# Value product of a recurrent attention kernel: four 32-column tiles instead of two 64-column tiles

## The chip, the cores and the metric

The kernel runs on one core of one Trainium2 chip. The metric is the device time of one execution in microseconds (us); the time before is 1757.63 us, the median of 3 runs (1756.89 to 1763.15). The core's engines are TensorE (PE in the profile, its weight loads PEld), VectorE (DVE), ScalarE (ACT), GpSimd (POOL) and SyncE (SP), which issues nearly all DMAs.

## The reference, cut to what matters

A gated sum of two branches over 2048 tokens of width 640: branch A is attention with a recurrent memory, branch B a gated feed-forward layer.

```python
def _A_ref(x, mem0, Wq, Wk, Wv, Wo, seg_len):     # 32 heads of 192, 8 memory rows, segments of 32 tokens
    mem = mem0
    for s in range(n_seg):                         # 64 segments
        xs = x[:, s * seg_len:(s + 1) * seg_len, :].copy()
        h = jnp.concatenate([mem, xs], axis=1)     # 40 rows
        q = jnp.einsum('btd,dhe->bhte', h, Wq)
        k = jnp.einsum('btd,dhe->bhte', h, Wk)
        v = jnp.einsum('btd,dhe->bhte', h, Wv)
        scores = jnp.einsum('bhqe,bhke->bhqk', q, k) * scale
        scores = jnp.where(mask[None, None], scores, -1000000000.0)
        p = _softmax(scores, axis=-1)
        o = jnp.einsum('bhqk,bhke->bhqe', p, v)    # the value product
        o = jnp.einsum('bhte,hed->btd', o, Wo)
        mem = o[:, :M, :].copy()
        outs.append(o[:, M:, :])
...
return g * a + (1 - g) * b
```

The memory rows of one segment come out of the segment before, so the 64 segments run one after another. All tensors are bf16.

## The kernel before

The kernel first computes the feed-forward branch in four blocks of 512 tokens and parks it in device memory, together with the columns of q and k that the last 8 tokens of each segment need. That ends at about 189 us of the profile. Then come the 64 segments of about 24.5 us each.

The weights of the attention do not all fit in the on-chip memory: in each segment a part of them is exchanged by loads on SP's queue (`load_piece`, L599), each of which waits until TensorE has done with what lies in the place.

The heads are worked in four groups of eight, called octets. `PROG` (L506) is an order written out by hand in which a segment's pieces follow one another on TensorE: projection steps `("g", n, k)`, transpositions of rows `("tq", o)` and `("tk", o)`, scores `("sc", o)`, softmax `("ex", o)`, transposition of the probabilities `("pt", o)`, value product `("pv", o)`, output projection `("wo", o, half)`, and pieces `("lf", ...)`, `("le", ...)`, `("vb", ...)` for the rows of later segments. Each engine runs its own list in that order; `_Sched.finalize` sets semaphore waits where a piece reads or writes what another engine wrote or read. If a TensorE piece has several waits, some are put ahead of the last matmuls of the piece before it.

Most matmuls of a segment use 32 of the 128 columns of the array: four stand side by side at column positions 0, 32, 64 and 96, each with its own moving data (projections L1046 and, with kept weights, L226; L884 and L1019 for the later segments' rows; the output projections L1206 and L1229; the transposition of the probabilities L1144 and L1149). The scores (L1087, L1095, L1100) have 40 columns and stand in two halves of 64.

The value product of an octet is `pv_oct` (L1165). Four pairs of heads lie in the partitions, and three parts `c` of 128 value columns each are multiplied with the transposed probabilities of two halves `i`: a wide matmul over all 160 columns (4 pairs x 40 rows, L1177) with the segment's own values `v`, and a narrow one of 64 columns (4 x 16, L1179) that adds the values `vl` of the last 8 tokens. Each takes 64 value columns as its weights, so two of them, `i` = 0 and 1, stand side by side in the array. That makes 12 matmuls and 12 weight loads per octet, 256 octets in all. Ahead of it stands ScalarE's evacuation of the transposed probabilities (L1162; for the last octet L1156 and L1158) and of the values (L1069). Behind it ScalarE evacuates the result (L1188; a third of the last octet goes to VectorE, L1193) for the output projection.

In the hand-written order the product of octet 0 lies between the scores of octet 1 and the transposition of octet 1; that of octet 1 directly behind the scores of octet 2 and ahead of the transposition of octet 2; that of octet 2 ahead of the scores of octet 3; that of octet 3 ahead of the last output projection, from whose result VectorE makes the memory rows of the next segment (L1371, L1375).

Of the kernel before, what the change touches and what calls it, by code (L numbers as in the profile page):

```python
# [231 lines left out]
def _build(nc, A_x, A_mem0, A_Wq, A_Wk, A_Wv, A_Wo, seg_len, w_gate, w_up, w_down,  # L232
# [18 lines left out]
    R = L + M  # L251
    XA = L - M
# [14 lines left out]
    S_ = _Sched(nc)  # L267
# [27 lines left out]
    NVB, NUB = 2, 2  # L295
# [33 lines left out]
    ps = nc.alloc_psum_tensor("ps", [128, 8, 512], F32)  # L329
# [3 lines left out]
    o = wsA_base - wsB_total  # L333
# [6 lines left out]
    o = wsA_base  # L340
# [4 lines left out]
    o = ffn_base  # L345
# [10 lines left out]
    def sreg(o, nbytes, plo=0, phi=128):  # L356
        return Rg("sb", o, o + nbytes, plo, phi)
# [39 lines left out]
    r_v = [sreg(wsB_off["v"] + b * 768, 768) for b in range(NVB)]  # L397
# [8 lines left out]
    PTm = PT[:, 0:PTW].rearrange("p (i t r) -> p i t r", t=4, r=R)  # L406
    PTl = PT[:, PTW:PTW + 128].rearrange("p (i t r) -> p i t r", t=4, r=16)
    r_PT = sreg(wsB_off["PT"], 2 * (PTW + 128))
# [23 lines left out]
    o = ffn_base - sum(fp_sz.values())  # L432
# [48 lines left out]
    r_ps = [Rg("ps", b, b + 1) for b in range(8)]  # L481
# [45 lines left out]
    def octet(s, i):  # L527
        return i if s % 2 == 0 else NOCT - 1 - i
# [35 lines left out]
    o = 0  # L564
# [71 lines left out]
    def load_residents(cls, pick=lambda key: True):  # L636
        for key in first:
# [7 lines left out]
           reads=[r_ident], writes=[r_ident])  # L645
    def asel(ap, reg, pattern, base, cm, fill):
# [12 lines left out]
           reads=[r_elw], writes=[r_elw])  # L659
# [19 lines left out]
    for h in range(NH):  # L679
        for w_, sb_, rw_, nm in ((w_gate, wg_sb, r_wg, "wg"), (w_up, wu_sb, r_wu, "wu")):  # L680
            S_.add("sp", lambda e, h=h, w_=w_, sb_=sb_: e.dma_start(
                sb_[h], w_.rearrange("(p k) f -> p k f", p=128)[:, :, FH * h:FH * (h + 1)]),
                writes=[rw_[h]], dma_sem="%s%d" % (nm, h))
# [228 lines left out]
    for n, (g, o) in enumerate(units):  # L912
# [7 lines left out]
        if g == 0:  # L920
            S_.add("pool", lambda e, o=o, b=b: e.tensor_copy(out=stg[o // 2][:, o % 2], in_=lst[b][:, 0]), reads=[r_lst[b]], writes=[r_stgh[o // 2][o % 2]],
                   name="stg s0 o%d" % o)
# [74 lines left out]
    def misc_bank(s, group=9):  # L997
        tick[0] += 1
        ok = [b for b in (0, 1, 2, 3) + ((LB,) if s % 4 in (1, 2) or s % 4 == 3 and group < 3 else ()) + ((OB,) if group < 2 else ()) if b not in bk_of.values() and b not in lb.values()]
        b = min(ok, key=lambda b: misc[b])  # L1000
        misc[b] = tick[0]
        return b

    def apx(ap, dims):
        return bass.AP(ap.tensor, ap.offset, [list(ap.ap[0])] + [list(d) for d in dims])
# [159 lines left out]
    def pv_oct(s, o):  # L1165
        A = misc_bank(s)
        B = misc_bank(s) if o in USPLIT else A
        oc = octet(s, o)
        v, vl, u = v_sb[o % NVB], vl_sb[oc], uT[o % NUB]
        ru = r_uTp[o % NUB]  # L1170
        W = 4 * R

        def half(c, i):
            full = ps[64 * i:64 * i + 64, B if c == 2 else A, W * c:W * c + W]
            part = full.rearrange("p (t r) -> p t r", r=R)[:, :, XA:R]
            e0 = 128 * c + 64 * i
            return [lambda e: e.matmul(full, v[:, e0:e0 + 64], PTm[:, i], start=True, stop=False,  # L1177
                                       tile_position=(0, 64 * i), skip_group_check=True),
                    lambda e: e.matmul(part, vl[:, e0:e0 + 64], PTl[:, i], start=False, stop=True,  # L1179
                                       tile_position=(0, 64 * i), skip_group_check=True)]  # L1180

        fns = [x for c in range(3) for y in zip(half(c, 0), half(c, 1)) for x in y]
        if s % 4 == 0:
            S_.add("pe", fns[:2], reads=[r_v[o % NVB], r_PT], writes=[r_ps[A]], name="PV s%d o%d" % (s, o))
            del fns[:2]
        S_.add("pe", fns, reads=[r_v[o % NVB], r_vl[oc], r_PT], writes=[r_ps[A]] + ([r_ps[B]] if B != A else []), name="PVa s%d o%d" % (s, o))
        na = 2 if o in USPLIT else 3
        S_.add("act", lambda e: e.activation(  # L1188
            out=apx(u[:, 0, 0, :], [[R, na], [3 * R, 4], [1, R]]),
            in_=ps[:, A, 0:na * W].rearrange("p (c t r) -> p c t r", t=4, r=R), func=ACTF.Copy),  # L1190
            reads=[r_ps[A]], writes=[ru[0]] if na == 2 else ru, name="uT evac s%d o%d" % (s, o))
        if na == 2:
            S_.add("dve", lambda e: e.tensor_copy(out=u[:, :, 2, :], in_=ps[:, B, 2 * W:3 * W].rearrange("p (t r) -> p t r", r=R)),  # L1193
                   reads=[r_ps[B]], writes=[ru[1]], name="uT mid s%d o%d" % (s, o))
        q = s % 4
        S_.add("pool", lambda e: e.tensor_copy(  # L1196
            out=uTl[:, 12 * oc:12 * oc + 12, M * q:M * q + M].rearrange("p (t c) i -> p t c i", c=3), in_=u[:, :, :, L:R]),
            reads=[r_uT[o % NUB]], writes=[r_uTl[oc]], name="uTl s%d o%d" % (s, o))
# [91 lines left out]
    def segment(s):  # L1290
# [3 lines left out]
        for n, item in enumerate(PROG):  # L1294
# [29 lines left out]
            elif kind == "pv":  # L1324
                pv_oct(s, i)
            elif kind == "lf":
                if i == q and unit(s, item[2]):
                    if item[3] == 0:
                        for m in range(2):
                            lb[item[2], m] = misc_bank(s)  # L1330
                    for m in range(2):
                        LBK[m] = lb[item[2], m]
                    left_mm(*unit(s, item[2]), item[3], unit_piece)
            elif kind == "vb":
                if q == 3 and g + 1 < NG:
                    if i == 0:
                        lb["v"] = misc_bank(s)
                    vl_mm(s + 1, i)
            elif kind == "le":
                if i == q and unit(s, item[2]):  # L1340
                    if n > n_wo:
                        post.append(item[2:])
                    else:
                        left_evac(s, *item[2:])
            else:
                held = wo_part(s, item)
                if i == 2 and item[2] == 0 and q == 0 and g > 0:
                    outl_store(g - 1)
                if item == items[-1] and s + 1 < NSEG:
                    stg_load(s + 1, 1)  # L1350
                if q == 3 and item != items[-1]:
                    wo_left(s, held)
# [118 lines left out]
```

## Time and profile before

| what | before |
|---|---|
| device time, median of 3 | 1757.63 us (1756.89 to 1763.15) |
| the profiled execution, span from first to last instruction | 1765.1 us (no other time of it is given) |
| mean granted TensorE clock | 0.994 |
| TensorE busy, matmuls | 1623.9 us, 92% |
| weight loads busy | 809.5 us, 46% |
| VectorE, ScalarE, GpSimd busy | 54%, 45%, 18% |
| value product, wide (L1177) | 1536 matmuls and weight loads, matmul mean 243 ns |
| value product, narrow (L1179) | 1536 matmuls and weight loads, matmul mean 193 ns |
| moved by DMA | 499.57 MB, mean 283 GB/s |

A matmul's own duration covers its way through the array, so successive matmuls overlap: four 384-wide matmuls side by side last 0.34 us each, and the next four start 0.16 us after them. For what a piece costs in TensorE's stream, the distance from start to start is to be read. A line of the timeline gives the start in us from the span's beginning, the time to the end of its group, engine, line, operation, the used rows and columns of the array, the moving operand, and how many; a bracket gives idle time of the engine before it and what ended it. "issue" in such a bracket means that the engine waited for nothing that the profile shows. In the page, the row "DMA" gives the busy share of the 16 DMA engines in tenths for 40 slices of the span, and the row that begins with "PE 71%" is the chain of work that ended last, by engine.

### The profile page before, as it was taken

To read this page: it belongs to the slowest core of one execution; us is meant where nothing else is said; L and a number is where in the kernel's file an instruction comes from. 1 tells how busy PE (TensorE), PEld (TensorE's weight loads), DVE (VectorE), ACT (ScalarE), POOL (GpSimd) and SP (SyncE) were. 2 spreads that over 40 slices of the span, in tenths; PEclk is the share of its full clock that TensorE was granted. 3 is DMA by queue.
4 is the path that set the end of the run, shared out by engine and by line. 5 is a ranking of instruction groups with operands and counts; after the bars stand their busy time and mean duration, and the time that the engine had idled before them with its cause. 6 is when DMAs were issued, how large, how long until landed. Compare 5 with 4: busy or idle time off the path is not lost.

```text
span 1765.1 us, 80301 instructions
## 1 busy us (share of the span) xinstructions
PE 1623.9 (92%) x39162; PEld 809.5 (46%) x31501; DVE 960.0 (54%) x2932; ACT 802.8 (45%) x1835; POOL 320.0 (18%) x1099
## 2 busy tenths in 40 slices
PE   9999999999999999999999989999999998999887
PEld 4554444444444444454444444454444444454444
DVE  2222655556555655555555655555555655655554
ACT  3222544545444544444444544444444544445443
POOL 1100111111112112111212111111211121121211
PEclk9999999999999999999999999999999999999999
DMA  9814987888778887888788887879787886879776
GB/s 335 295 48 157 329 313 250 320 313 288 280 269 311 299 308 253 315 290 319 281 280 293 296 293 250 314 285 323 279 280 275 311 310 241 312 282 327 283 275 238
DMA packets 271311, 499.57 MB, mean 283 GB/s; under 512 B 105304, under 2 KB 132208, under 8 KB 270960
## 3 DMA queue, kind: packets, MB, share of 16 engines
q1 hardware_dynamic: 267832, 491.34, 78.3%
q8 instruction: 276, 4.52, 1.0%
q10 hardware_dynamic: 3128, 3.09, 0.6%
q14 instruction: 75, 0.61, 0.1%
HBM read 473.22 MB, written 21.11 MB: 280 GB/s over the span
## 4 chain that ended last, share of the span: by engine, by line
PE 71%; DVE 15%; DMA 6%; issue 4%; ACT 4%; DVEq 0%; SPq 0%; ACTq 0%
PE ps L1046 20%; PE ps L226 15%; PE ps L1206 8%; DMA arena<-in_A_Wo_dram 5%; PE ps L1177 3%; PE ps L804 3%; PE ps L801 3%; PE ps L884 3%; PE ps L1100 3%; PE ps L819 2%; PE ps L1087 2%; DVE ps L1114 2%; DVE arena L1112 2%; PE ps L1095 2%; PE ps L1229 2%
## 5 line engine op out<-in xcount | busy, mean ns | idle before, releaser
L1046 PE MATMUL ps<-arena 128*32 128x384 bf16 x9940 | 723.0, 329 | 42.4 <-DVE arena L1375 34.4
L226 PE MATMUL ps<-arena 128*32 128x384 bf16 x7680 | 595.4, 328 | 7.9 <-DVE arena L1215 3.5
L1046 PEld LDWEIGHTS ps<-arena 128*32 128x32 bf16 x9940 | 257.5, 97 | 365.3 <-issue 226.0
L1080 DVE STREAM_TRANSPOSE arena<-arena 128x384 bf16<-128x384 bf16 x512 | 270.8, 557 | 150.8 <-ACT arena L1066 149.2
L1066 ACT ACTIVATE arena<-ps 128x384 bf16<-128x384 f32 x512 | 236.2, 489 | 211.6 <-PE ps L1046 196.3
L1206 PE MATMUL ps<-arena 128*32 128x320 bf16 x6144 | 293.6, 301 | 13.9 <-issue 13.4
L1124 ACT ACTIVATE ps<-ps 104x160 f32<-104x160 f32 x256 | 71.9, 281 | 293.4 <-DVE ps L1114 293.4
L1206 PEld LDWEIGHTS ps<-arena 128*32 128x32 bf16 x6144 | 163.5, 97 | 74.0 <-issue 19.4
L1112 DVE TENSOR_REDUCE arena<-ps 104x4 f32<-104x160 f32 x256 | 83.0, 324 | 165.8 <-PE ps L1100 164.6
L941 POOL COPY arena<-arena 128x96 bf16<-128x96 bf16 x256 | 70.3, 275 | 513.4 <-PE ps L1100 444.2
L1188 ACT ACTIVATE arena<-ps 128x480 bf16<-128x480 f32 (+1 forms) x256 | 137.0, 535 | 43.8 <-PE ps L1179 39.6
L1196 POOL COPY arena<-arena 128x96 bf16<-128x96 bf16 x256 | 68.3, 267 | 441.1 <-ACT arena L1188 357.3
L1162 ACT ACTIVATE arena<-ps 128x448 bf16<-128x448 f32 x192 | 104.2, 543 | 96.7 <-PE ps L1149 96.4
L1069 ACT ACTIVATE arena<-ps 128x384 bf16<-128x384 f32 x256 | 125.1, 489 | 20.9 <-PE ps L1046 16.3
L1177 PE MATMUL ps<-arena 128*64 128x160 bf16 x1536 | 123.1, 243 | 12.5 <-ACT arena L1162 6.9
L1126 DVE TENSOR_REDUCE arena<-ps 104x4 f32<-104x160 f32 x256 | 83.0, 324 | 92.5 <-ACT ps L1124 92.5
L1177 PEld LDWEIGHTS ps<-arena 128*64 128x64 bf16 x1536 | 80.8, 109 | 91.6 <-issue 31.7
L884 PE MATMUL ps<-arena 128*32 128x384 bf16 x1280 | 111.4, 330 | 2.2 <-issue 2.0
L1179 PE MATMUL ps<-arena 128*64 128x64 bf16 x1536 | 104.8, 193 | 4.1 <-issue 4.1
L891 DVE STREAM_TRANSPOSE arena<-arena 128x384 bf16<-128x384 bf16 x128 | 73.7, 576 | 31.6 <-ACT arena L889 27.8
L1215 DVE TENSOR_TENSOR arena<-ps,arena 64x160 f32<-64x160 f32 x160 | 50.8, 317 | 72.3 <-ACT arena L1212 61.6
L1114 DVE TENSOR_TENSOR ps<-ps,arena 104x160 f32<-104x160 f32 x256 | 85.0, 332 | 8.8
(84 smaller groups left out, 1819.2 us busy)
## 6 DMA issues: line engine op xcount, KB each, us to landing
arena<-in_A_Wk_dram SPq DMA_DIRECT2D x335, 384.0 KB, 7.1
arena<-in_A_Wv_dram SPq DMA_DIRECT2D x335, 384.0 KB, 9.1
arena<-in_A_Wo_dram SPq DMA_DIRECT2D x205, 480.0 KB, 6.4
arena<-in_A_Wq_dram SPq DMA_DIRECT2D x209, 384.0 KB, 5.4
arena<-left_qk_scratch SPq DMA_DIRECT2D x126, 96.0 KB, 2.8
left_qk_scratch<-arena SPq DMA_DIRECT2D x49, 192.0 KB, 2.3
left_qk_scratch<-arena SPq DMA_DIRECT2D x30, 96.0 KB, 5.7
ffn_b_scratch<-arena ACTq DMA_DIRECT2D x16, 160.0 KB, 4.4
```

Source lines behind the costliest of these rows:

```text
L226: return e.add_instruction(mybir.InstMatmult(name=nm, start_tensor_calc=like["start"], stop_tensor_calc=stop, tile_size=(128, 32), tile_po ...
L884: fns.append(lambda e, outp=outp, rhs=rhs, j=j: e.matmul(outp, lhs, rhs, start=(k == 0), stop=(k == KT - 1), tile_position=(0, 32 * j)))
L1046: fns.append(lambda e, outp=outp, rhs=rhs, j=j: e.matmul(outp, lhs, rhs, start=(k == 0), stop=(k == KT - 1), tile_position=(0, 32 * j)))
L1066: S_.add("act", lambda e, m=m, bk=bk: e.activation(out=rows_sb[m], in_=ps[:, bk, 0:384], func=ACTF.Copy), reads=[r_ps[bk]], writes=[r_rows ...
L1069: S_.add("act", lambda e, i=i, bk=bk: e.activation(out=v_sb[i % NVB].rearrange("p (c n) -> p c n", c=3), in_=ps[:, bk, 0:384].rearrange("p ...
L1080: S_.add("dve", lambda e: e.transpose(out=dst[:, :, 0:L], in_=rows_sb[m].rearrange("p (c r) -> p c r", r=L)), reads=[r_rows[m]], writes=[r ...
L1112: S_.add("dve", lambda e: e.tensor_reduce(out=mxs, in_=S3, axis=AX.X, op=ALU.max), reads=[rb], writes=[rst], name="smax max")
L1114: S_.add("dve", lambda e: e.tensor_tensor(out=S3, in0=S3, in1=mxb, op=ALU.subtract), reads=[rb, rst], writes=[rb], name="smax sub")
L1177: return [lambda e: e.matmul(full, v[:, e0:e0 + 64], PTm[:, i], start=True, stop=False, tile_position=(0, 64 * i), skip_group_check=True), ...
L1179: lambda e: e.matmul(part, vl[:, e0:e0 + 64], PTl[:, i], start=False, stop=True, tile_position=(0, 64 * i), skip_group_check=True)]
L1188: S_.add("act", lambda e: e.activation(out=apx(u[:, 0, 0, :], [[R, na], [3 * R, 4], [1, R]]), in_=ps[:, A, 0:na * W].rearrange("p (c t r) ...
L1206: fns.append(lambda e, i=i, t=t, j=j, gv=gv: e.matmul(ps[32 * j:32 * j + 32, bank, 0:2 * DJ].rearrange("p (h n) -> p h n", h=2), lhs2[i], ...
```

## The change

In `pv_oct` the two 64-column tiles of each matmul become four 32-column tiles. Each part `c` now issues four wide matmuls, at column positions 0, 32, 64 and 96, and then four narrow ones; the moving operand and the place in the result are unchanged, the weights are 32 value columns each. An octet has 24 matmuls and 24 weight loads. In segments whose number is a multiple of four the first piece, which doesn't wait for `vl`, holds four matmuls instead of two. No other function is touched, and the other engines' instructions keep their order.

```diff
-        def half(c, i):
-            full = ps[64 * i:64 * i + 64, B if c == 2 else A, W * c:W * c + W]
-            part = full.rearrange("p (t r) -> p t r", r=R)[:, :, XA:R]
-            e0 = 128 * c + 64 * i
-            return [lambda e: e.matmul(full, v[:, e0:e0 + 64], PTm[:, i], start=True, stop=False,
-                                       tile_position=(0, 64 * i), skip_group_check=True),
-                    lambda e: e.matmul(part, vl[:, e0:e0 + 64], PTl[:, i], start=False, stop=True,
-                                       tile_position=(0, 64 * i), skip_group_check=True)]
-
-        fns = [x for c in range(3) for y in zip(half(c, 0), half(c, 1)) for x in y]
+        def strips(c):
+            full, part = [], []
+            for i in range(2):
+                for h in range(2):
+                    lo = 64 * i + 32 * h
+                    acc = ps[lo:lo + 32, B if c == 2 else A, W * c:W * c + W]
+                    e0 = 128 * c + lo
+                    full.append(lambda e, acc=acc, e0=e0, i=i, lo=lo: e.matmul(
+                        acc, v[:, e0:e0 + 32], PTm[:, i], start=True, stop=False, tile_position=(0, lo), skip_group_check=True))
+                    part.append(lambda e, acc=acc, e0=e0, i=i, lo=lo: e.matmul(
+                        acc.rearrange("p (t r) -> p t r", r=R)[:, :, XA:R], vl[:, e0:e0 + 32], PTl[:, i], start=False, stop=True,
+                        tile_position=(0, lo), skip_group_check=True))
+            return full + part
+
+        fns = [x for c in range(3) for x in strips(c)]
         if s % 4 == 0:
-            S_.add("pe", fns[:2], reads=[r_v[o % NVB], r_PT], writes=[r_ps[A]], name="PV s%d o%d" % (s, o))
-            del fns[:2]
+            S_.add("pe", fns[:4], reads=[r_v[o % NVB], r_PT], writes=[r_ps[A]], name="PV s%d o%d" % (s, o))
+            del fns[:4]
```

## The prediction

> **What bounds the kernel now.** I read the page first: the busy shares, the DMA and queue rows, the chain.
>
> ```profile
> span 1765.1 us, 80301 instructions
> PE 1623.9 (92%) x39162; PEld 809.5 (46%) x31501; DVE 960.0 (54%) x2932; ACT 802.8 (45%) x1835; POOL 320.0 (18%) x1099
> ...
> DMA  9814987888778887888788887879787886879776
> ...
> q8 instruction: 276, 4.52, 1.0%
> ...
> PE 71%; DVE 15%; DMA 6%; issue 4%; ACT 4%; DVEq 0%; SPq 0%; ACTq 0%
> ```
>
> TensorE is busy in 92% of the span and holds 71% of the chain: what shortens its stream counts unless something else ends the wait. The q8 row matters as much. In it 276 packets carry 4.52 MB. 39162 matmuls and 31501 weight loads are 70663 instructions, 256.0 to each of the 276 packets: the stream comes in 16 KB blocks of 256, so more instructions mean more blocks.
>
> Then the timeline of PE, around one value product and around one transposition of the probabilities.
>
> ```profile
> 926.58 0.34 PE L226 MATMUL ps<-arena 128*32 128x384 bf16 x4
> 926.85 0.26 PE L1177 MATMUL ps<-arena 128*64 128x160 bf16 x2
> 926.94 0.20 PE L1179 MATMUL ps<-arena 128*64 128x64 bf16 x2
> 926.97 0.24 PE L1177 MATMUL ps<-arena 128*64 128x160 bf16 x2
> 927.04 0.20 PE L1179 MATMUL ps<-arena 128*64 128x64 bf16 x2
> 927.07 0.24 PE L1177 MATMUL ps<-arena 128*64 128x160 bf16 x2
> 927.14 0.20 PE L1179 MATMUL ps<-arena 128*64 128x64 bf16 x2
> 927.27 0.35 PE L1046 MATMUL ps<-arena 128*32 128x384 bf16 x4
> 927.44 0.34 PE L226 MATMUL ps<-arena 128*32 128x384 bf16 x4
> ```
>
> ```profile
> 903.54 0.34 PE L226 MATMUL ps<-arena 128*32 128x384 bf16 x4
> 903.70 0.21 PE L1144 MATMUL ps<-arena 104*32 104x80 bf16 x4
> 903.74 0.23 PE L1149 MATMUL ps<-arena 104*32 104x128 bf16 x4
> 903.80 0.34 PE L1046 MATMUL ps<-arena 128*32 128x384 bf16 x4
> ...
> 907.26 0.22 PE L1144 MATMUL ps<-arena 104*32 104x80 bf16 x4 [0.30 <-DVE arena L1131]
> ```
>
> Four 32-column matmuls of 384 take 0.16 us from group to group, and a 32-column group of another kind (L1144) starts at that distance too. The 64-column L1177 starts 0.27 us after L226, and L1046 0.13 us after the last L1179, though 64 columns cost only 0.03 us between the pairs. So changing the tile's width costs about 0.1 us each way. L1144 at 907.26 waits for VectorE's softmax: an earlier TensorE gains nothing there.
>
> Last, a gap named "issue".
>
> ```profile
> 470.53 0.24 PE L1177 MATMUL ps<-arena 128*64 128x160 bf16 x1
> 472.21 0.26 PE L1177 MATMUL ps<-arena 128*64 128x160 bf16 x1 [1.44 <-issue]
> ```
>
> TensorE stops 1.44 us inside the value product, waiting for no semaphore. From 189 us on there are 55 such gaps over 30 ns, 34.7 us together. Counted along matmuls and weight loads they lie multiples of 256 apart: those at 466.0, 472.2, 523.6 and 547.7 us stand before instructions 14746, 15002, 17306 and 18330, in four different lines. TensorE waits there for the next block. All other idle time of TensorE there is 94 us.
>
> **The change part by part.** I work in distances between starts, medians over the trace, in ns; 256 value products (64 segments, four octets).
>
> *Removed: the width changes.* Last matmul before to first L1177: 256 after a 384-wide group, against 153 between two such groups: 103 lost. The product of octet 1 follows the scores (L1100) at 106, and from L1100 to the 32-column L1046 it is 106 too, so nothing is won there. Last L1179 to the next group 122, against 25 from L1179 to L1177: 97 lost.
>
> *The block.* First to last start is now 298. The new block is three 160-wide and three 64-wide groups of four. A four-group of 160 exists (L1229: 3+3+3+59, so 68); the 64-wide one lies between 27 (64/384 of the 160 that a 384-wide group takes) and 35 (25 plus three starts). So the block to the next start costs 3 x 68 + 3 x 27..35 = 285 to 309; I take 300. Now that part is 298 + 122 = 420: 120 saved (111 to 135), plus 103 on entry for three of four octets. A segment saves 3 x 223 + 120 = 789, and 64 of them 50 us (48 to 54).
>
> *What does not reach the end.* The third octet's transposition waits for VectorE in 58 of 64 segments (23.8 us): octet 1's product lies between that octet's scores and this wait, so 58 x 0.12 = 7 us vanish. 15 products of octet 2 wait for ScalarE (L1162) and drain meanwhile: 1.5. The later transpositions wait 48 times, and take perhaps half of octet 2's saving: 5. Left 36, I take 35; bounds 25 and 50. Octet 3's product feeds a serial chain (evacuation, Wo), so its saving passes on. The wait that each product has on ScalarE or VectorE stands before the same first matmul; with four in that first piece instead of two nothing new queues behind it. No transfer and no instruction of the other engines moves.
>
> *Added: instructions.* 12 matmuls and 12 weight loads per product are 24 x 256 = 6144 instructions, 24 blocks: 276 to 300. A segment goes from 1060 instructions (4.14 blocks) to 1156 (4.52). Lower bound: each block stalls as now, 34.7 us / 253 = 0.14 us, 24 x 0.14 = 3 us. But stalls depend on how long a block lasts. The packet records of q8 in the trace put the start of the fetch of the next block 2.9 us (median) after the running block's first instruction when the 16 DMA engines are full, 1.1 us when they are nearly idle; the next block's first instruction runs at least 2.36 us after that start. A block that lasts under some 5.3 us with DMA full is thus in danger. The 149 blocks that begin with DMA full, sorted by duration without the stall:
>
> - under 4.8 us: 7 blocks, all stalled, mean 1.35 us
> - 4.8 to 5.2: 31, mean 0.33
> - 5.2 to 5.6: 35, mean 0.14
> - 5.6 to 6.0: 60, mean 0.05
> - longer: 16, mean 0.05
>
> The sum is 28.5 us. With 1060/1156 of the old work and 35 of 1570 us saved, a block lasts 0.90 of what it did, and there are 1.09 times as many. The rows move down a class: 8 x 1.8 + 34 x 1.35 + 38 x 0.6 + 65 x 0.2 + 17 x 0.1 = 98 us (the values between classes read off the list, 1.8 extrapolated). That is +69; a tenth falls where TensorE would have waited anyway: +62. Upper bound 100 (all 162 blocks at 0.8 us, less the 28.5). I take 62, not 3: the list is this kernel's own behaviour at the durations that the blocks will have.
>
> On this the Trainium skill says otherwise: Runtime: NRT & Kernel Launch, Instruction fetch mechanics, has the next 16 KiB block fetched while the present one runs and the crossing "mostly hidden". By it the sum would end at the 35 us saved; the 55 gaps speak against it.
>
> *Sum.* -35 + 62 = +27 us. On the profiled execution's span, 1765.1 (the page gives no other time of it, and it is 0.4% above the median of the runs), that is 1792; on the median 1757.63 it is 1785.
>
> **The rivals.**
>
> *The fetch stays hidden (faster).* Place: the block boundaries; price: -35 + 3 = -32 us, so 1726. For it: the fetch starts at 1.1 us when DMA is idle, and a stall of TensorE lets DMA run dry, so stalls may limit themselves; boundaries also fall elsewhere in the program. Against it: DMA is nine tenths busy in most slices and the short blocks all stall. It decides when the stalls grow by less than 35 us, under about 0.25 us for each block.
>
> *They cancel.* Stalls grow by 27 to 43 us: 1749 to 1766.
>
> *A floor for each matmul (slower still).* If every matmul took 25 ns, the product would last 600 instead of 300: 153 + 600 against 256 + 298 + 122, +77 ns, 20 us on 256, and with less dense blocks perhaps 20 us of new stalls: 1798. For it: L1095's two-tile pairs of 40 columns take 28 ns, not 17. Against it: L1144's four start 3 ns apart and the next group 0.04 us after the first.
> TensorE: Matmul & The Clock Gate (the Trainium skill), Wait — 56ns, not 53.3ns?, states that floor of about 25 ns between starts; the L1144 rows, four tiles side by side, do not show it.
>
> *The drain does not belong to the width* and stays: then only the block changes, nothing is saved, and +55 us of stalls gives 1813. Against it: L1144's undelayed start.
>
> **How the numbers follow.** Stalls outgrow the saving: 0.54, likeliest 1785, own range 1767 to 1812. Fetch hidden: 0.23, 1726, 1710 to 1749. Cancel: 0.13. Floor 0.05, drain stays 0.05. A measurement of this kernel can tell about 0.5% (8.8 us) from no change: slower 0.54 + 0.05 + 0.05 = 0.64, same 0.13, faster 0.23. The range leaves a tenth out at either end: half of the faster case, below 1729, and the top of the slower ones, above 1815.
>
> **What would show it.** In the profile after: 42234 matmuls, 34573 weight loads, q8 with 300 packets and 4.92 MB. The product from the group before to the group after: about 0.45 us where it was 0.68. Gaps named issue: near 97 us where they were 34.7, again 256 instructions apart, most in the stretches where DMA is full. The third transposition's wait longer by about 0.1 us. It is wrong if those gaps stay under 70 us, or if L1144 and Wo wait so little that stalls of TensorE pass on in full.

## The result

The changed kernel takes 1834.8 us (median of 4 runs, 1828.99 to 1835.47) against 1760.39 us for the kernel before beside it: a ratio of 1.0398, 95% interval 1.0354 to 1.0443. It is 74 us slower. The forecast was slower, 1785 us, with a range from 1729 to 1815: the direction and the mechanism came out, the size did not.

The rows of the page that answer to those shown of the kernel before:

```profile
span 1833.7 us, 86445 instructions
PE 1606.6 (88%) x42234; PEld 830.1 (45%) x34573; DVE 959.2 (52%) x2932; ACT 804.8 (44%) x1835; POOL 321.6 (18%) x1099
...
DMA  9816887878777877878777887878777887778786
...
q8 instruction: 300, 4.92, 1.1%
...
PE 69%; DVE 16%; issue 9%; ACT 4%; DMA 1%; DVEq 0%; SPq 0%; ACTq 0%
```

TensorE is busy 17 us less than before, in a span that is 69 us longer. The instruction queue q8 has its 24 blocks more, and "issue" went from 4% of the chain to 9%.

The timeline of PE around one value product of the changed kernel (L1180 is the wide matmul, L1182 the narrow one):

```profile
913.35 0.34 PE L226 MATMUL ps<-arena 128*32 128x384 bf16 x4
913.52 0.34 PE L1046 MATMUL ps<-arena 128*32 128x384 bf16 x4
913.68 0.24 PE L1180 MATMUL ps<-arena 128*32 128x160 bf16 x4
913.75 0.20 PE L1182 MATMUL ps<-arena 128*32 128x64 bf16 x4
913.78 0.24 PE L1180 MATMUL ps<-arena 128*32 128x160 bf16 x4
913.85 0.20 PE L1182 MATMUL ps<-arena 128*32 128x64 bf16 x4
913.88 0.24 PE L1180 MATMUL ps<-arena 128*32 128x160 bf16 x4
913.95 0.20 PE L1182 MATMUL ps<-arena 128*32 128x64 bf16 x4
913.97 0.34 PE L1046 MATMUL ps<-arena 128*32 128x384 bf16 x4
```

The product now starts 0.16 us after the group before it, as any group does, lasts 0.29 us to the next group, and the next group follows at once. From the start of the group before to the start of the group after it takes 0.45 us, as forecast, where it was 0.69 in the kernel before. On the array the change does just what the start distances promised.

The waits of TensorE's matmuls, longest first (us in total, times, longest):

```profile
PE ps L1046 <- DVE arena L1380: 34.0, 48, 1.4
PE ps L1211 <- issue: 23.1, 25, 1.7
PE ps L1144 <- DVE arena L1131: 22.8, 48, 0.8
PE ps L1182 <- issue: 20.6, 15, 2.4
PE ps L1046 <- issue: 19.9, 19, 1.8
PE ps L1180 <- issue: 11.1, 13, 1.5
PE ps L884 <- issue: 10.3, 11, 1.6
```

The same view of the kernel before had, for comparison:

```profile
PE ps L1046 <- DVE arena L1375: 34.4, 48, 1.2
PE ps L1144 <- DVE arena L1131: 25.0, 65, 0.7
PE ps L1206 <- issue: 13.4, 14, 2.0
...
PE ps L1229 <- DMA arena<-in_A_Wo_dram: 6.1, 10, 2.3
PE ps L1046 <- issue: 5.4, 8, 1.3
PE ps L1177 <- issue: 4.8, 6, 1.5
PE ps L1179 <- issue: 4.1, 6, 1.3
```

The waits for VectorE (L1380, in the old numbering L1375, and L1131) are about what they were; the wait for the weights Wo (L1229) is gone. What grew is "issue": in the product (old L1177 and L1179, new L1180 and L1182), but also in the projections (L1046, L884) and the output projection (old L1206, new L1211), which the change did not touch. From 189 us on these gaps are 116.7 us in 130 places, where they were 34.7 us in 55; again they stand multiples of 256 instructions apart.

A gap shows less than what a late block costs. In the changed kernel:

```profile
918.87 0.34 PE L1046 MATMUL ps<-arena 128*32 128x384 bf16 x3
920.01 0.34 PE L1046 MATMUL ps<-arena 128*32 128x384 bf16 x1 [0.81 <-issue]
```

The fourth matmul of a group starts 1.13 us after the third, where it normally starts 0.003 us after it; the gap is 0.81 us, because the third's own 0.34 us are still counted as work. So I count a stall at each block boundary as the start distance there, less the median distance of the same pair of lines elsewhere. Added up over the segments by the place in the segment (us from VectorE's L975, or the same line in the other kernels, which ends a segment's output; all stalls over 0.06 us):

```
                0-10   10-14  14-18  18-22  22-     sum
before           4.9     4.4   23.3   24.7    1.6    59
after            9.1    45.8   53.7   35.1   15.5   159
```

The 16 DMA engines are full (a mean share of 0.9 to 1.0 over the segments) from about 2.5 to 18 us of a segment in both kernels, then fall to 0.8 at 19 us, 0.5 at 21 us and 0.2 from 22 us on. The stalls have grown by 100 us, 72 of them at 10 to 18 us. Those that stand later mostly follow blocks that were entered earlier: 93% of the stall time in the changed kernel, and 91% in the kernel before, lies behind blocks in whose first 3 us the DMA engines are over 0.9 busy. (Such blocks are called blocks that begin with DMA full in what follows.) The span has grown by 68.6 us, so everything else together has become 32 us shorter.

The packets of q8 tie these stalls to the fetch. In the changed kernel the next block's packet starts 3.1 us (median) after a block that begins with DMA full is entered, and 1.1 us after it where DMA is under 0.2 busy; the packet itself takes 1.0 us in both. It is the start that is late. At the 118 boundaries with a stall of more than 0.5 us the first matmul runs 2.4 us (median, nine tenths between 2.3 and 2.6) after the start of the last packet: the end of the stall follows the packet at an almost fixed distance.

### The profile page after: what moved, and what is told of

It reads as the page before. It is cut to its first block, busy times and chain, and to the rows that moved or that the text cites. A ratio compares the mean times of both kernels' runs of the same rounds, so it can differ in the third digit from the quotient of the medians.

```text
span 1833.7 us, 86445 instructions
## 1 busy us (share of the span) xinstructions
PE 1606.6 (88%) x42234; PEld 830.1 (45%) x34573; DVE 959.2 (52%) x2932; ACT 804.8 (44%) x1835; POOL 321.6 (18%) x1099
## 4 chain that ended last, share of the span: by engine, by line
PE 69%; DVE 16%; issue 9%; ACT 4%; DMA 1%; DVEq 0%; SPq 0%; ACTq 0%
PE ps L1046 18%; PE ps L226 14%; PE ps L1211 9%; PE ps L884 3%; PE ps L804 3%; PE ps L1100 3%; PE ps L801 3%; PE ps L1180 3%; DVE ps L1114 2%; PE ps L1087 2%; DVE arena L1112 2%; PE ps L1095 2%; PE ps L819 2%; DVE arena L1126 2%; DVE arena L891 2%
## 5 line engine op out<-in xcount | busy, mean ns | idle before, releaser
L1046 PE MATMUL ps<-arena 128*32 128x384 bf16 x9940 | 733.1, 328 | 55.7 <-DVE arena L1380 34.0
L226 PE MATMUL ps<-arena 128*32 128x384 bf16 x7680 | 602.7, 327 | 16.4 <-ACT arena L1193 6.7
L1046 PEld LDWEIGHTS ps<-arena 128*32 128x32 bf16 x9940 | 266.9, 97 | 364.2 <-issue 234.9
L1211 PE MATMUL ps<-arena 128*32 128x320 bf16 x6144 | 314.4, 307 | 24.8 <-issue 23.1
L1211 PEld LDWEIGHTS ps<-arena 128*32 128x32 bf16 x6144 | 177.9, 98 | 87.2 <-issue 30.3
L1180 PE MATMUL ps<-arena 128*32 128x160 bf16 x3072 | 125.3, 236 | 18.9 <-issue 11.1
L1182 PE MATMUL ps<-arena 128*32 128x64 bf16 x3072 | 112.3, 194 | 20.7 <-issue 20.6
L884 PE MATMUL ps<-arena 128*32 128x384 bf16 x1280 | 120.7, 331 | 10.4 <-issue 10.3
L1180 PEld LDWEIGHTS ps<-arena 128*32 128x32 bf16 x3072 | 83.7, 96 | 69.7 <-issue 20.5
L1144 PE MATMUL ps<-arena 104*32 104x80 bf16 x1024 | 63.2, 207 | 39.9 <-DVE arena L1131 22.8
L1182 PEld LDWEIGHTS ps<-arena 128*32 128x32 bf16 x3072 | 82.0, 97 | 28.9 <-issue 23.2
```

The lines of the kernel that those rows point to most:

```text
L226: return e.add_instruction(mybir.InstMatmult(name=nm, start_tensor_calc=like["start"], stop_tensor_calc=stop, tile_size=(128, 32), tile_po ...
L884: fns.append(lambda e, outp=outp, rhs=rhs, j=j: e.matmul(outp, lhs, rhs, start=(k == 0), stop=(k == KT - 1), tile_position=(0, 32 * j)))
L1046: fns.append(lambda e, outp=outp, rhs=rhs, j=j: e.matmul(outp, lhs, rhs, start=(k == 0), stop=(k == KT - 1), tile_position=(0, 32 * j)))
L1180: full.append(lambda e, acc=acc, e0=e0, i=i, lo=lo: e.matmul(acc, v[:, e0:e0 + 32], PTm[:, i], start=True, stop=False, tile_position=(0, l ...
L1182: part.append(lambda e, acc=acc, e0=e0, i=i, lo=lo: e.matmul(acc.rearrange("p (t r) -> p t r", r=R)[:, :, XA:R], vl[:, e0:e0 + 32], PTl[:, ...
L1211: fns.append(lambda e, i=i, t=t, j=j, gv=gv: e.matmul(ps[32 * j:32 * j + 32, bank, 0:2 * DJ].rearrange("p (h n) -> p h n", h=2), lhs2[i], ...
```

## The experiments

Theory A is the prediction's: the time comes from blocks of 256 instructions that are fetched too late while DMA is full. Theory B: four 32-column tiles are slow by themselves. Theory C came up on the way: TensorE's stream is not what ends the time, and what is saved in it goes into waits; in the runs on weight loads it says besides that instructions count only beyond their old number. All ratios are to runs of the kernel before on the same chip.

### The same number of instructions, without the tiles, in two places

Both kernels keep the 64-column value product and cut 32 projection matmuls of each segment into four pieces of a quarter of the columns, with kept weights: 6144 matmuls more, as many instructions as the change adds. They differ in one number, the projection group that is cut. Only the calls are shown; the cutting itself, in `mms`, is left out:

```diff
-            S_.add("pe", mms(m, bk, htile(k), k, g_, n > 0),
+            S_.add("pe", mms(m, bk, htile(k), k, g_, n > 0, 4 if k and item[1] == 4 else 1),   # split_full
+            S_.add("pe", mms(m, bk, htile(k), k, g_, n > 0, 4 if k and item[1] == 0 else 1),   # split_idle
```

> The kernel before, with its 64-column value product. In the fifth projection group (values of octet 2, queries of octet 3), steps k = 1 to 4, each of the 32 matmuls of 384 columns is cut into four of 96 with kept weights: 96 matmuls more in each segment, no weight load, the same columns through the array, the result unchanged. That is exactly as many instructions as the change adds (6144, 24 blocks of 256), placed where the 16 DMA engines are full. Theory A (the time comes from fetching instruction blocks while DMA is full): stalls at block boundaries grow as in the changed kernel, from 53 us to 120 to 150 us counted by start distances, and with nothing saved the time is 1830 to 1865 us; q8 has 300 packets. Theory B (four 32-column tiles in the value product are slow by themselves, in weight loads or in writing the result; the number of instructions does not matter): at most 1770 us, the 10 us being the array's own cost of the cut.

> The same cut with the same 96 extra matmuls in each segment, but in the first projection group (queries and keys of octet 0), where a segment begins and the DMA engines are partly idle (0.3 to 0.7 busy before the segment's loads have built up). Theory A: a fetch there starts 1.1 us after the running block begins instead of 2.9, so the same 24 blocks cost a third or less: 1765 to 1800 us, clearly under split_full. Theory A without the DMA part (each block costs the same wherever it lies): the same time as split_full within 10 us. Theory B: 1760 to 1770 us, like split_full.

split_full: 1872.37 us, ratio 1.0626 (1.059 to 1.0662). It is 7 us over the upper end of theory A's range. split_idle: 1768.88 us (10 runs, 1765.59 to 1779.78), ratio 1.0057 (1.0032 to 1.0083). Two rows of each page, first split_full:

```profile
q8 instruction: 300, 4.92, 1.1%
...
PE 73%; DVE 12%; issue 9%; ACT 3%; DMA 2%; DVEq 0%; SPq 0%; ACTq 0%
```

And split_idle:

```profile
q8 instruction: 300, 4.92, 1.1%
...
PE 73%; DVE 14%; DMA 5%; issue 5%; ACT 4%; DVEq 0%; SPq 0%; ACTq 0%
```

```
stalls          0-10   10-14  14-18  18-22  22-     sum
split_full      14.7    90.3   34.0   14.8   12.8   167
split_idle       5.8    15.0   23.4   20.3    5.4    70
```

The same 24 blocks cost 112 us in one place and 8 us in the other. Where they stand in split_full, at 10 to 14 us of a segment, the stalls went from 4.4 to 90.3 us. The loss does not need the tiles of theory B: no value product was touched here. Nor is it the number of blocks alone: it is blocks that run short while DMA is full. In split_idle 40 of the 41 blocks that begin with DMA under 0.3 busy pass in under 5.2 us, and they are followed by 2 us of stalls together. split_idle came out at the low end of theory A's range, with its stalls 11 us above the kernel before, and theory B's range for it held the time too; split_full is what tells the two apart.

### Fewer bytes in flight

In both kernels every load that exchanges weights during the segments moves only the first quarter of its columns. The rest of the place keeps old weights, so the results lack the new ones; all instructions and waits stay. The edit, shortened:

```diff
+            if name.startswith("swap"):
+                dst, src = [x[:, :, 0:Dm // 4] if key[0] == 3 else x[:, 0:OW // 4] for x in (dst, src)]
```

> The kernel before, but each load that exchanges weights during the segments moves only the first quarter of its columns; the rest of the place keeps the weights that lay there, so the result is not the reference's. All instructions and waits stay. Theory A (a block's fetch is late because DMA is full): the 16 engines are no longer full anywhere in a segment, stalls at block boundaries fall from 60 us to 5 to 25 us by start distances, and the time to 1700 to 1735 us. Theory A without the DMA part (a block costs what it costs): within 10 us of the kernel before, less some 6 us of waits on loads.

> The changed kernel with the same quarter loads, so again not the reference's result. Theory A: with the fetches in time the saving of the 32-column tiles is what is left: 25 to 50 us under before_light, stalls under 35 us. If the 6144 instructions cost by themselves, or the four tiles do (theory B): 30 to 75 us above before_light, as with the full loads.

before_light: 1704.23 us, ratio 0.9707 (0.968 to 0.9734). after_light: 1692.7 us, ratio 0.9636 (0.9606 to 0.9665). The pages, before_light first:

```profile
DMA  9923733434334342434333343333333333334332
...
q8 instruction: 276, 4.52, 1.1%
...
PE 74%; DVE 17%; ACT 5%; issue 3%; DMA 0%; DVEq 0%; SPq 0%; ACTq 0%
```

```profile
DMA  9923733434334342434333343334333333334332
...
q8 instruction: 300, 4.92, 1.2%
...
PE 69%; DVE 21%; ACT 6%; issue 4%; DMA 0%; DVEq 0%; ACTq 0%
```

With the DMA engines a third busy the stalls are 12 us in before_light and 13 us in after_light: 24 blocks more cost 1 us. The order of the two kernels turns round, and the change is 11.5 us faster: neither the 6144 instructions nor the four tiles are slow by themselves. Short blocks are not late by themselves either: in after_light 177 of 288 blocks pass in under 5.2 us, with 4 us of stalls behind them. That bears out theory A. What the packet waits behind, the DMA engines or the memory that they read, is not told apart by these runs. The pair also shows that the saving was overestimated: 25 to 50 us were expected, 11.5 came. In after_light TensorE is 28 us less busy and idles 18 us more than in before_light; 10 us of the latter are at the transposition of the probabilities, where it waits for VectorE's softmax (30.6 us in before_light and 40.6 in after_light, gaps down to 0.03 us counted), and 9 us in waits for the evacuation of the product, for the output projection and for the keys. Theory C is right to that extent. The view of waits, which leaves out short gaps, has for that transposition, before_light first:

```profile
PE ps L1150 <- DVE arena L1137: 29.2, 76, 0.7
```

```profile
PE ps L1150 <- DVE arena L1137: 36.7, 75, 0.8
```

The Trainium skill (Runtime: NRT & Kernel Launch, Instruction fetch mechanics) holds that crossing a 16 KiB block boundary is mostly hidden. The light pair agrees, at 0.04 us a block; with DMA full the trace does not, at 0.21 us a block in the kernel before (59 us in 276 blocks) and 0.53 in the changed one (159 in 300).

### Tiles at the old number of instructions

The narrow matmuls are left out, so the results lack the values of the last 8 tokens. wide_only has 32-column tiles and the old number of instructions; wide_only_64 has 64-column tiles and 3072 instructions fewer. In both, the wide matmul now ends its sum (`stop=True`). Shortened:

```diff
-            return full + part
+            return full                                                    # wide_only
-            return [lambda e: e.matmul(full, ...), lambda e: e.matmul(part, ...)]
+            return [lambda e: e.matmul(full, ...)]                          # wide_only_64
```

> The changed kernel without its narrow matmuls: the value product leaves out the part that adds the last 8 tokens' values (vl), so the result lacks it. 12 matmuls and 12 weight loads for each octet, as many as before the change, but in 32-column tiles. Theory A: the width changes are gone and the number of instructions is the old one, so the saving shows: 36 us from the tiles and some 15 to 20 us from the three narrow groups of 28 ns that are left out, 1690 to 1725 us. Theory B: 32-column tiles cost as much per matmul as they do in the changed kernel; half of them are gone, so 1760 to 1800 us.

> The kernel before, in 64-column tiles, without its narrow matmuls (the values of the last 8 tokens are left out of the result, as in wide_only): 6 matmuls and 6 weight loads for each octet, 3072 instructions and 12 blocks fewer than before. The array does 3 x 28 ns less for each octet and keeps both width changes. Theory A: 12 blocks fewer where DMA is full are worth 2 to 4.5 us each (24 cost 103 us of stalls in the changed kernel), so stalls fall by 20 to 45 us and the time is 1700 to 1740 us, under wide_only, though wide_only has 50 us less work on the array. Theory C (TensorE's stream is not what ends the time here, waits for VectorE and ScalarE take up what is saved, as wide_only's 1765 us could also be read): 1750 to 1765 us.

wide_only: 1765.25 us, ratio 1.0005 (0.9985 to 1.0025), no difference, where theory A forecast 1690 to 1725; it lies in theory B's range, 1760 to 1800. wide_only_64: 1744.59 us, ratio 0.9911 (0.987 to 0.9952), faster by 14 us, between theory A's range (up to 1740) and theory C's (from 1750). The waits in wide_only:

```profile
PE ps L1144 <- DVE arena L1131: 38.3, 83, 0.8
PE ps L1046 <- DVE arena L1380: 33.1, 48, 1.3
PE ps L1211 <- issue: 15.6, 14, 2.3
PE ps L1180 <- issue: 13.7, 13, 1.9
```

```
stalls          0-10   10-14  14-18  18-22  22-     sum
wide_only        5.8    13.2   29.2   29.2    5.0    83
wide_only_64     4.6     0.9    6.9   18.5    0.0    31
```

TensorE's work in wide_only is 45 us less by the page (1578.9 us busy against 1623.9), so the tiles are not slow, as theory B has it; but nothing of the saving reaches the end. Stalls are 24 us more, though not one instruction was added: where the product stands, the same 256 instructions now pass in less time, and more blocks are due before their fetch is done. Of the blocks that begin with DMA full 69 of 175 last under 5.2 us without their stall, against 46 of 173 in the kernel before. TensorE's idle time for VectorE grows from 76 to 99 us. So about half of the saving goes into late blocks, as in theory A, and half into waits for VectorE, as in theory C. wide_only_64 leaves TensorE 25 us more work than wide_only and is 21 us faster: its stalls are 52 us fewer. So here the number of instructions counts more than the array's time. The miss in wide_only is in part that of the prediction: I treated a saving on the array as if it left the fetches alone, and as if nearly all of it passed the waits.

### The change for one octet

The edit, shortened; `half` and `strips` are the two forms of the product in the diff above:

```diff
+        thin = o in (3,)
+        fns = [x for c in range(3) for x in strips(c)] if thin else [x for c in range(3) for y in zip(half(c, 0), half(c, 1)) for x in y]
```

> The change in the last octet of each segment only: 24 more instructions in each segment, in its last third, where DMA runs empty; octets 0 to 2 keep 64-column tiles. Theory A: 64 x 0.22 us = 14 us saved, six blocks more of which most are fetched with DMA low, so 1735 to 1757 us. Theory B: a quarter of the whole change, 1770 to 1785 us.

1777.53 us, ratio 1.0096 (1.006 to 1.0132): 1% slower, inside theory B's range and above theory A's, which was my forecast. The stalls are 85 us, 26 more than before, and 13.5 of them lie from 22 us on, where the kernel before has 1.6. So the source is again the stalls, which theory B does not have. Octet 3's product lies mostly at 20 to 22 us of a segment, where DMA is emptying; but the blocks behind which these late stalls stand were nearly all entered at 17 to 19 us, with DMA over 0.8 busy. I had put the empty stretch too early. Why the rest, 14 us, stands in other places was not tried; the six blocks move every later boundary of the program.

### Fewer weight loads

Projection groups 1 and 3 run their k steps backwards, so that the next group's first step finds its weights still in the array: 956 weight loads fewer, the result unchanged. Shortened:

```diff
+    def kstep(item):
+        return KT - 1 - item[2] if item[1] in (1, 3) else item[2]
+        held = step == 0 and item[1] in (1, 2, 3, 4) and not prev
-            S_.add("pe", mms(m, bk, htile(k), k, g_, n > 0),
+            S_.add("pe", mms(m, bk, htile(k), k, g_, n > 0 or held),
```

> The kernel before with 956 weight loads fewer (3.7 blocks) and no other work changed: projection groups 1 and 3 run their five k steps backwards, so that the first step of groups 1 to 4 needs the weights that the group before has just used, and keeps them. The result is unchanged. Theory A (blocks fetched while DMA is full end the time): 3.7 blocks at 1 to 4.3 us each (4.3 is what a block more cost in the changed kernel), stalls 45 to 56 us instead of 60, time 1742 to 1756 us. Theory C (the instruction count matters only when it is above the old one, and TensorE's stream ends nothing else): no difference, 1757 to 1762 us.

> The changed kernel with the same 956 weight loads fewer. Theory A: where half the blocks stall, a block is dearer, 2.5 to 6 us: 1812 to 1826 us, and still above the kernel before. Theory C: 1800 us or less if the number of instructions only counts beyond a threshold, or the changed kernel's 1834 us if it does not count.

> As keep_weights, and the last projection group (values of octet 3) runs its five k steps backwards too. In keep_weights the pieces of Wv that are exchanged after group 1 came in the order k = 4 to 0 and were asked for in the order 0 to 4 in group 6, and 33 us of waits on loads of Wv stood there that the kernel before does not have. Now the order of asking is that of loading. Theory A: those waits go to under 5 us, the idle time named issue stays near 27 us, where it is 34.7 before, and the time is 1738 to 1754 us, the first kernel here under the one before with its result unchanged. Theory C: 1757 to 1762 us.

keep_weights: 1777.18 us, ratio 1.0101 (1.0075 to 1.0127), 1% slower, above the ranges of both theories. Its longest waits on TensorE:

```profile
PE ps L1052 <- DVE arena L1381: 34.4, 48, 0.9
PE ps L1052 <- DMA arena<-in_A_Wv_dram: 33.0, 34, 2.1
```

The second line is new: pieces of Wv now arrive in another order than the last group asks for them. "issue" fell to 27 us. keep_weights_order turns that group round as well: 1760.32 us, ratio 0.9991 (0.9973 to 1.0009), no difference: theory C's forecast (1757 to 1762), and a miss for theory A (1738 to 1754). The wait on Wv is gone, but "issue" is back at 36 us and the stalls are 65 us. So the 27 us were no gain of the fewer loads; more likely TensorE, held up by Wv, gave the fetches time. The loads that were dropped stand at the seams of groups 0 to 4, most of them in the first 8 us of a segment, and early blocks hardly stall (4.9 us up to 10 us in the kernel before). That four blocks fewer there are worth nothing fits this, as 24 more there cost little in split_idle.

change_keep_weights, the same on the changed kernel: 1812.63 us, ratio 1.0304 (1.0268 to 1.0341), 22 us under the changed kernel, at the low end of theory A's range; stalls 130 us. Nearly all of the 29 us fewer stalls lie from 14 us of a segment on, not where the loads were dropped, and TensorE waits 11.6 us for Wv here too. So how much of the 22 us the fewer loads are worth is not shown, and the place alone does not explain why the same loads are worth nothing in keep_weights_order. That instructions count only beyond their old number does not fit the other runs: before_light has the old number and is 54 us faster with its stalls nearly gone, and wide_only_64, with fewer, has half the stalls. No version with an unchanged result beat the kernel before.

## Why the prediction was right or wrong

- *The width changes and the block.* Right. 0.45 us from group to group where 0.45 was forecast, and no extra time on either side.
- *The number of instructions.* Right: 42234 matmuls, 34573 weight loads, 300 blocks.
- *The cause.* Right, and now shown: split_full makes the loss without the tiles, split_idle has the instructions almost without the loss, the light pair turns the sign, and the stalls end 2.4 us after the start of a q8 packet.
- *"+62 us" of stalls.* This is the term that failed, the growth of the stalls: it measured 100 us by start distances, 82 us in gaps. The list of blocks was made from gaps, which leave out part of each stall (1.13 us against 0.81 in the example above), so the 28.5 us that it started from were too few (59 by start distances, all blocks counted). The upper bound of 100 was made from the same gaps. The tenth that I took off for stalls ahead of waits was no more than a guess; the two waits that the prediction names at its end, at the transposition (25.0 us before, 22.8 after) and for Wo (6.1 us, then none), gave up 8 us. And the list took all blocks to be 0.90 as long, where the change packs its added instructions into the stretch in which the products stand (6 to 22 us of a segment): the median block that begins with DMA full went from 5.46 to 4.70 us without its stall, to 0.86. Of these blocks 46 of 173 lasted under 5.2 us in the kernel before, 144 of 188 in the changed one.
- *"-35 us" of saving.* Open for the full kernels, and too large where it could be measured. With the fetches in time (the light pair) only 11.5 us reach the end: of the 50 us that the blocks save, some 38 vanish in waits there, where I had let 14 vanish. The remainder of the span in the full kernels, -32 us, looks like the forecast, but that is no proof of it: it holds other things too, such as the waits on loads that are gone (6.7 us in the kernel before). In the full kernels saving and stalls can't be told apart, since a stall ahead of a wait is not paid twice: -11.5 us with 86 of the 100 us of stalls, or -26 us with all of them, give the same 74 us.
- *The rivals.* "The fetch stays hidden" is what the light pair shows and the full kernel does not. "They cancel" is out. The floor of 25 ns for each matmul is out: 24 matmuls pass in 0.29 us, 12 ns each. The drain does belong to the width.
- *The third transposition's wait*, forecast longer by 0.1 us in each segment, does not show in the changed kernel: all transpositions together wait 25.0 us for this VectorE line before and 22.8 after. The stalls ahead of it are the likely reason: in after_light, without them, the wait is 10 us longer.

## What to carry to other kernels

This kernel's instructions come as 16 KB packets, 276 before and 300 after, on a queue of the same DMA engines that carry its data. In such a kernel, where the engines are full, look at the idle time named "issue", see whether it comes every so many instructions, and treat instructions as a cost like array time: here 24 blocks cost 112 us in one place and 8 us in another. Measure such a stall by start distances, not by gaps, and test a saving on TensorE with the suspected stall taken away before counting on it.

## What the runs showed of the hardware that was not expected

The same 6144 matmuls are worth 6.3% or 0.6% of the kernel's time, depending on whether they stand where DMA is full (split_full) or half busy (split_idle). In both traces the packet of a 16 KB block of instructions takes about 1.0 us; with DMA full it starts 3.1 us (median) after the block before is entered, with DMA under 0.2 busy 1.1 us. A saving of 45 us of TensorE's busy time at an unchanged number of instructions (wide_only) was worth nothing: about half of it came back as 24 us more of late blocks, and 23 us as longer waits for VectorE.
